# Unit 2's queries in halves, a cast on GpSimd, and the third and fourth piece of w_out ahead of v

## The chip, the cores and the metric

The kernel runs on one core of a Trainium2 chip. The metric is the device time of one execution in microseconds (us), taken as the median over runs. Engines are named as in the profile: PE (TensorE; PEld is its weight load), DVE (VectorE), ACT (ScalarE), POOL (GpSimd), SP (SyncE, which here only issues transfers).

## The reference

Two operators follow one another. The first is a recurrent retention over 4 batches, 8 heads, 768 steps, head size 64; the second is a feed-forward layer with a leaky rectifier over the 3072 x 512 result.

```python
state = gamma * state + einsum('bhd,bhe->bhde', k[:, :, t], v[:, :, t])
y[:, :, t] = scale * einsum('bhd,bhde->bhe', q[:, :, t], state)
...
h = x @ w_in                                             # 3072x512 @ 512x2048
g = np.maximum(h, 0.0) + alpha * np.minimum(h, 0.0)
return (g @ w_out).astype(np.float32)                    # 3072x2048 @ 2048x512
```

Inputs and output are float32.

## The kernel before

**Tiling.** Time is cut into units of 256 steps, three to a batch, twelve in all (u = 0 to 11). Two units make a block of 512 tokens, six in all (n = 0 to 5). The feed-forward layer works on blocks. All matmuls take float16.

**A unit.** `load` brings its k, q and v into staging tiles. `rescale` multiplies k (t = 0) and q (t = 1) with powers of the decay into the tile `kdq`; `cast_v` writes v as `vx`. `turn_pe(u, hh, bank)` transposes `kdq` for four of the eight heads (hh = 0: heads 0 to 3), four transposes of k and then four of q, and ACT copies the result to `kq` (line 236). `score_mm(u, hh, banks)` multiplies k with q into two banks, and `masks` writes the masked scores from there on DVE (line 482). `sum_mm` forms the unit's contribution to the state from `kdq` and `vx` (line 260). `state` adds it to the running state on DVE (`ss`), decays it on POOL (`tf`) and copies it to `tg` on POOL and ACT. `out_mm` forms y out of `tg` (line 500) and out of scores and `vx` (line 532), and `take_y` copies y as `xT`, the input of the feed-forward layer.

**A block.** `ffn1(n, ...)` multiplies `xT` with w_in into `hps` (line 629) and applies the rectifier on ACT and DVE (lines 640, 642). `ffn2(0, ..., parts=4)`, block 0's second product, multiplies the result with w_out into four banks (line 798). Both are generators: `tick(gen, m)` emits the next m matmuls, so matmuls of the layer stand between the steps of the units. `ffn2` has 64 matmuls. They go in four rounds over slices of four of w_out's sixteen row tiles; in each round every one of the four banks gets four matmuls. So matmuls 0 to 15 read row tiles 0 to 3, matmuls 16 to 31 read row tiles 4 to 7, where each group of four goes through the slice.

**w_in and w_out.** w_in comes in pieces of float32 (`get_wi`) which POOL casts (`cast_wi`). w_out's first half comes in four pieces of two row tiles, 512 KB each (`get_wo32(0)` to `(3)`), cast by `cast_wo(engine, i)` on the engine given. Pieces 2 and 3 land where w_in's columns of tiles 4 to 7 lay, so their loads wait until these are cast. The second half comes by transfers that POOL issues (`get_wo(2)`, `get_wo(3)`, line 971). The loads of unit 4's queries and everything behind them on SP wait for `get_wo(2)` to land.

**What sets the order.** The order is written out by hand in lines 986 to 1284: each engine runs its instructions in the order in which the program emits them, and waits at each for what it needs. All loads named above but `get_wo` are issued by SP, in program order, and each issue waits until its destination is free.

**Around the change.** While PE ends block 0's first product, POOL casts the last pieces of w_in, scales unit 2's k in two halves (27.64 to 29.68 us) and its q in one, and casts its v. Then PE goes through `tick(gen, 5)`, the turn of heads 0 to 3 of unit 2, six ticks, scores, the turn of heads 4 to 7, six ticks, scores, state sums, eight ticks, `out_mm(2)`, seven ticks, and goes on to `half`, block 1's first product (lines 1097 to 1124).

The loads of units 0 and 1 already come in halves, by part names such as "k0" and "k1": heads 0 to 3 and heads 4 to 7.

Of the kernel before, what the change touches and what calls it, by code (L numbers as in the profile page):

```python
# [22 lines left out]
def kernel(  # L23
# [76 lines left out]
    def ps(bank, name, dt=FP, n=512):  # L100
        return psp.tile([128, n], dt, tag=f"b{bank}", name=name)
# [27 lines left out]
    def hold(ins):  # L129
        if held:  # L130
            tc.add_manual_dep(
                ins.ins,
                held.pop().ins.name,
                mybir.DependencyInfo(
                    mybir.DependencyClass.Sync, mybir.DependencyReason.DATA
                ),
                reason="loads behind weights",
            )

    def rows(x):  # L140
        return slice(64 * x, 64 * x + 64)

    def load(u, parts="kqv"):
        if u >= NU:
            return
        b, c = divmod(u, UPB)
        t = staged.setdefault(u, {})
        for nm in parts:
            src = {"k": k, "q": q, "v": v}[nm[0]]
            if nm[0] not in t:  # L150
                t[nm[0]] = sbp.tile(
                    [128, H, 2 * D], FP, tag=f"{nm[0]}s", bufs=3, name=f"{nm[0]}s{u}"
                )
            h = slice(0, H) if len(nm) == 1 else slice(4 * int(nm[1]), 4 * int(nm[1]) + 4)
            if u >= SPLIT and nm != "q":
                for x in range(2):
                    for y in range(2):
                        at = U * c + 128 * x + 64 * y
                        nc.sync.dma_start(
                            out=t[nm][rows(x), :, D * y : D * y + D],  # L160
                            in_=src[b, :, at : at + 64, :].rearrange("h p d -> p h d"),
                        )
                continue
            hold(
                nc.sync.dma_start(  # L165
                    out=t[nm[0]][:, h, :],
                    in_=src[b, h, U * c : U * c + U, :].rearrange(
                        "h (p r) d -> p h (r d)", r=2
                    ),
                )  # L170
            )

    def unit(u):
        if u not in prepped:
            prepped[u] = (
                sbp.tile([128, 2, 2, H, D], F16, tag="kdq", bufs=3, name=f"kdq{u}"),
                sbp.tile([128, 4 * NP, 128], F16, tag="kq", bufs=3, name=f"kq{u}"),
                sbp.tile([128, H, 2, D], F16, tag="vx", bufs=3, name=f"vx{u}"),
            )
        return prepped[u]  # L180

    def rescale(eng, u, t, h0, h1):
        kdq = unit(u)[0]
        at = OQ if t else (O2 if u >= SPLIT else 0)
        return eng.tensor_tensor(  # L185
            out=kdq[:, t, :, h0:h1, :].rearrange("p r h d -> p h r d"),
            in0=staged[u]["kq"[t]][:, h0:h1, :].rearrange("p h (r d) -> p h r d", r=2),
            in1=tab[:, at + 2 * h0 : at + 2 * h1]
            .rearrange("p (h r) -> p h r", r=2)
            .unsqueeze(3)  # L190
            .to_broadcast([128, h1 - h0, 2, D]),
            op=MULT,
        )
# [28 lines left out]
    def turn_pe(u, hh, bank):  # L222

        kdq, kq, _ = unit(u)
        trb = ps(bank, "trb", F16, 1024)
        n = 0
        for t in range(2):
            for r in range(2):
                for p in (2 * hh, 2 * hh + 1):
                    nc.tensor.transpose(  # L230
                        out=trb[:, n : n + 128],
                        in_=kdq[:, t, r, 2 * p : 2 * p + 2, :].rearrange("p a d -> p (a d)"),
                        identity=ident,
                    )
                    n += 128
        nc.scalar.activation(  # L236
            out=kq.rearrange("p (x a) i -> p x a i", x=4)[:, :, 2 * hh : 2 * hh + 2, :],
            in_=trb.rearrange("p (x a i) -> p x a i", x=4, a=2),
            func=COPY,
            bias=0.0,  # L240
            scale=1.0,
        )

    def qmove(kq, a, c, p):
        return kq.rearrange("p (t r a) i -> p t r a i", t=2, r=2)[rows(a), 1, :, p, rows(c)]
# [207 lines left out]
    def score_mm(u, hh, banks):  # L453
        _, kq, _ = prepped[u]
        kv = kq.rearrange("p (t r a) i -> p t r a i", t=2, r=2)
        scs = [ps(banks[0], "sca"), ps(banks[1], "scb")]
        for r in range(2):
            for pp in range(2):
                p = 2 * hh + pp
                for c in range(2):  # L460
                    for a in range(2):
                        at, n, q = 256 * r + 128 * pp, 128, qmove(kq, a, c, p)
                        if u >= SPLIT and r == 1:
                            at, n, q = 256 + 64 * pp, 64, q[:, :, 32:64]
                        nc.tensor.matmul(  # L465
                            out=scs[a][rows(c), at : at + n],
                            lhsT=kv[rows(a), 0, r, p, rows(c)],
                            rhs=q,
                            start=True,
                            stop=True,  # L470
                        )
        live[u, hh] = scs

    def masks(u, hh, parts=(0, 1)):
        for a in parts:
            m2 = sbp.tile([128, 512], F16, tag=f"m2{a}{hh}", bufs=2, name=f"m2{a}{hh}")
            if u >= SPLIT:
                i = nc.vector.tensor_tensor(
                    out=m2[:, 0:384], in0=live[u, hh][a][:, 0:384], in1=mj, op=MULT
                )  # L480
            else:
                i = nc.vector.tensor_tensor(  # L482
                    out=m2.rearrange("p (r a i) -> p r a i", r=2, a=2),
                    in0=live[u, hh][a].rearrange("p (r a i) -> p r a i", r=2, a=2),
                    in1=mask.unsqueeze(2).to_broadcast([128, 2, 2, 128]),
                    op=MULT,
                )
            live[u, hh][a] = m2
        return i
# [458 lines left out]
    def tick(gen, m=10**6):  # L948
        for _ in range(m):
            if next(gen, 1) == 1:  # L950
                return
# [4 lines left out]
    def win_part(lo, hi):  # L956
        x, y = ((1, 0), (1, 1), (0, 0), (1, 0))[lo // 4]
        return early[x][:, y, :, 128 * (lo % 4) : 128 * (hi - lo + lo % 4)]
# [4 lines left out]
    def cast_wi(eng, lo, hi):  # L963
        o, i = w_in_all[:, :, 128 * lo : 128 * hi], win_part(lo, hi)
        if eng is nc.scalar:
            return eng.activation(out=o, in_=i, func=COPY, bias=0.0, scale=1.0)
        return eng.tensor_copy(out=o, in_=i)  # L967
# [5 lines left out]
    def wo_part(i):  # L973
        return early[i // 2][:, 1, 2 * (i % 2) : 2 * (i % 2) + 2, :]

    def get_wo32(i):
        nc.sync.dma_start(out=wo_part(i), in_=wo[:, 2 * i : 2 * i + 2, :])  # L977

    def cast_wo(eng, i):
        o, i = w_out_all[:, 2 * i : 2 * i + 2, :], wo_part(i)  # L980
        if eng is nc.scalar:
            return eng.activation(out=o, in_=i, func=COPY, bias=0.0, scale=1.0)
        return eng.tensor_copy(out=o, in_=i)  # L983


    V, G, A = nc.vector, nc.gpsimd, nc.scalar
# [79 lines left out]
    load(2, ("k0", "k1"))  # L1066
    get_wo32(0)
    get_wo32(1)
    load(2, ("q", "v"))
    score_mm(1, 1, (0, 1))  # L1070
    masks(1, 1)
    state(1, 1, V)
    gen = ffn1(0, (2, 3, 6, 7, 0, 1, 2, 3, 6, 7, 4, 5, 0, 1, 2, 3), apart=4)
# [2 lines left out]
    cast_wi(G, 6, 8)  # L1076
    get_wo32(2)
    get_wo32(3)
    cast_wi(G, 8, 10)
    cast_wi(G, 10, 12)  # L1080
    cast_wi(G, 12, 14)
    cast_wi(G, 14, 16)
    rescale(G, 2, 0, 0, 4)
    rescale(G, 2, 0, 4, 8)
    rescale(G, 2, 1, 0, 8)
    load(3, ("k", "q", "v"))
    cast_v(G, 2)
    out_mm(1, (4, 5), evict=False)
# [7 lines left out]

    gen = ffn2(0, (0, 1, 2, 3), parts=4)
    half = ffn1(1, (6, 7, 4, 5, 4, 6, 0, 1, 2, 3, 0, 4, 5, 6, 7, 1), apart=12)
    tick(gen, 5)
    turn_pe(2, 0, 5)  # L1100
    tick(gen, 6)
    score_mm(2, 0, (6, 7))
    masks(2, 0)
    cast_wo(V, 2)
    cast_wo(V, 3)
    wsum = sbp.tile([128, 4, HF, HM], F16, tag="wsum", name="wsum")
    turn_pe(2, 1, 4)
    tick(gen, 6)
    score_mm(2, 1, (6, 7))
    sum_mm(2, (5, 4))  # L1110
    state(2, 0, G, "ga")
# [6 lines left out]
    get_wo(3)  # L1118
    cast_v(G, 3)
    w_sums(0, 0, HF, G)  # L1120
    tick(gen, 8)
    out_mm(2, (4, 5))
    tick(gen, 7)
    tick(half, 24)
    turn_pe(3, 0, 6)
    tick(half, 8)
# [39 lines left out]
    for n in range(1, NBLK):  # L1166
        more = n + 1 < NBLK
        u0 = 2 * (n + 1)
        if n > 1:
            if more:  # L1170
                gen = ffn1(n, (7, 2, 3, 1, 0, 6, 5, 4, 7, 1, 0, 4, 5, 6, 7, 1))
            else:
                gen = ffn1_mixed(n, PLAN5, BANKS5)
# [21 lines left out]
        gen = ffn2_seven(n, 0, 1) if more else ffn2_seven(n, 0, 1, (2, 3, (4, 6)))  # L1195
# [119 lines left out]
```

## Time and profile before

| | |
|---|---|
| median of 3 runs | 201.85 us (201.05 to 202.13) |
| profiled execution | 200.61 us, of which span 198.6 us |
| PE busy | 189.7 us (95%) |
| DVE, ACT, POOL busy | 157.6, 115.1, 104.2 us |
| granted TensorE clock | 1.00 |
| HBM read, written | 27.31 MB, 6.29 MB |

The span is the time between the first and the last instruction of the profiled execution; the execution takes 2.0 us more. Times in the rows are us from the start of the span. In the order in time a row gives start, length, engine, line, operation, output and inputs, count, and in brackets the idle time of the engine ahead of it and what ended it. In a row on transfers stand the destination and source, the issuing queue, count, KB each, and the us from issue to landing. Matmuls are pipelined, so that the length of a row of matmuls reaches beyond the start of the next. DMA shares count the packets' own time.

### The profile page before, as it was taken

The page shows a single profiled execution, that of the slowest core. Times are in us where ns is not written, and L with a number is a line of the kernel's source. Part 1 is how long each engine was busy: PE and PEld are TensorE (multiplying, and loading weights), DVE is VectorE, ACT ScalarE, POOL GpSimd, SP SyncE. Part 2 cuts the span into 40 slices and gives each one's busy share as a digit, 9 for nine tenths or more (in the row PEclk, how much of TensorE's full clock was granted, in tenths as well). Part 3 has the DMA queues.
Part 4 walks back from the last instruction along what each step waited for, and adds up shares of the span by engine and source line. Part 5 has one row for each costly group of instructions (what it writes and reads, how often), then busy time and mean ns, then how long its engine had stood idle before and what let it go on. Part 6 is the DMA issues. An engine that isn't in the chain of part 4 may idle for free.

```text
span 198.6 us, 6058 instructions
## 1 busy us (share of the span) xinstructions
PE 189.7 (95%) x2517; PEld 127.8 (64%) x2517; DVE 157.6 (79%) x261; ACT 115.1 (58%) x198; POOL 104.2 (52%) x110
## 2 busy tenths in 40 slices
PE   6788997999999999999999999999999999999993
PEld 2456543468458598744688644688644788865882
DVE  7798986626698998289989289987389998899983
ACT  4465665338267568466557567467467476678110
POOL 3298685099468634981067990076970181039300
PEclk9999999999999999999999999999999999999999
DMA  5999999987969998899897999918966010400014
GB/s 160 324 328 338 376 375 331 323 164 124 237 144 243 262 174 224 201 314 231 170 220 182 306 187 216 237 59 220 270 111 131 17 56 3 158 3 0 0 61 150
DMA packets 90009, 37.90 MB, mean 191 GB/s; under 512 B 57968, under 2 KB 87680, under 8 KB 89984
## 3 DMA queue, kind: packets, MB, share of 16 engines
q1 hardware_dynamic: 88752, 36.45, 69.8%
q0 software_dynamic: 1056, 1.05, 3.5%
q8 instruction: 19, 0.31, 0.6%
q10 hardware_dynamic: 176, 0.04, 0.2%
q14 instruction: 6, 0.05, 0.1%
HBM read 27.31 MB, written 6.29 MB: 169 GB/s over the span
## 4 chain that ended last, share of the span: by engine, by line
PE 83%; DVE 5%; DMA 4%; SPq 3%; ACT 1%; POOL 1%; issue 1%; DVEq 0%
PE hps L629 28%; PE ox L846 16%; PE oy L846 13%; PE ops L798 6%; DMA qs<-in_q_dram 4%; PE hps L712 3%; PE sp L752 3%; DVE m L482 2%; PE kps L106 2%; SPq L165 2%; PE y L532 1%; PE sca L465 1%; PE st L284 1%; POOL kdq L185 1%; PE trb L230 1%; SPq L977 1%
## 5 line engine op out<-in xcount | busy, mean ns | idle before, releaser
L629 PE MATMUL hps<-xT,win 128*128 128x512 f16 (+1 forms) x384 | 70.9, 344 | 0.3 <-POOL win L967 0.3
L642 DVE SCALAR_TENSOR_TENSOR gt<-hm,oma,hps 128x512 f16<-128x512 f32 (+1 forms) x96 | 59.1, 656 | 13.6 <-ACT hm L640 5.1
L640 ACT ACTIVATE hm<-hps 128x512 f32<-128x512 f32 x80 | 47.4, 596 | 25.2 <-PE hps L629 22.8
L629 PEld LDWEIGHTS <-win 128*128 128x128 f16 x384 | 37.1, 98 | 31.8 <-POOL win L967 0.8
L846 PEld LDWEIGHTS <-gs 128*128 128x128 f16 x320 | 31.0, 98 | 3.7
L846 PEld LDWEIGHTS <-gt 128*128 128x128 f16 x240 | 22.9, 98 | 4.2
L185 POOL TENSOR_TENSOR kdq<-qs,tab 128x1024 f16<-128x1024 f32 (+1 forms) x11 | 20.0, 1822 | 5.7 <-DMA qs<-in_q_dram 3.4
L333 POOL CAST tg<-tm 64x256 f16<-64x256 f32 x12 | 4.8, 396 | 33.6 <-DVE tm L301 22.6
L185 POOL TENSOR_TENSOR kdq<-ks,tab 128x1024 f16<-128x1024 f32 (+1 forms) x12 | 20.2, 1686 | 3.6 <-PE y L514 2.6
L555 ACT ACTIVATE xT<-y 128x512 f16<-128x512 f32 x22 | 14.9, 743 | 4.6 <-PE y L532 3.4
L846 PE MATMUL ox<-wout,gt 128*128 128x256 f16 x144 | 17.3, 273 | 0.0
L846 PE MATMUL oy<-wsum,gs 128*128 128x256 f16 x144 | 17.2, 273 | 0.0
L798 PE MATMUL ops<-wout,gt 128*128 128x512 f16 x64 | 15.5, 380 | 0.4 <-DVE wout L983 0.4
L201 POOL CAST vx<-vs 128x1024 f16<-128x1024 f32 (+1 forms) x13 | 12.6, 970 | 5.3 <-DMA vs<-in_v_dram 5.3
L612 DVE TENSOR_TENSOR gs<-gt 128x1024 f16<-128x1024 f16 (+1 forms) x14 | 13.0, 934 | 0.2
L236 ACT ACTIVATE kq<-trb 128x1024 f16<-128x1024 f16 x8 | 8.2, 1023 | 7.0 <-PE trb L230 7.0
L866 ACT ACTIVATE cu<-oy 128x512 f32<-128x512 f32 x10 | 6.0, 597 | 10.7 <-PE oy L846 10.1
L313 POOL TENSOR_TENSOR tf<-ss,tab 128x256 f32<-128x256 f32 x10 | 10.3, 1028 | 2.5 <-DVE ss L312 1.5
L662 POOL TENSOR_SCALAR hn<-qc,oma 128x256 f32<-128x256 f32 x4 | 4.5, 1140 | 12.5 <-DVE qc L774 12.4
L423 POOL TENSOR_TENSOR tf<-ss,tab 128x256 f32<-128x256 f32 x6 | 5.8, 974 | 9.6 <-DVE ss L422 9.6
L870 DVE TENSOR_TENSOR os<-ox,cu 128x512 f32<-128x512 f32 x5 | 3.4, 686 | 9.1 <-PE ox L846 9.1
L967 POOL CAST win<-early 128x1024 f16<-128x1024 f32 (+1 forms) x9 | 8.8, 975 | 2.4 <-DMA early<-in_moe_w_in_dram 2.2
(118 smaller groups left out, 289.7 us busy)
## 6 DMA issues: line engine op xcount, KB each, us to landing
qs<-in_q_dram SPq DMA_DIRECT2D x10, 512.0 KB, 5.1
ks<-in_k_dram SPq DMA_DIRECT2D x32, 128.0 KB, 3.5
vs<-in_v_dram SPq DMA_DIRECT2D x32, 128.0 KB, 4.3
early<-in_moe_w_in_dram SPq DMA_DIRECT2D x7, 512.0 KB, 8.3
out_dram<-os SPq DMA_DIRECT2D x9, 256.0 KB, 2.7
early<-in_moe_w_out_dram SPq DMA_DIRECT2D x4, 512.0 KB, 6.7
out_dram<-ot SPq DMA_DIRECT2D x4, 512.0 KB, 4.1
ks<-in_k_dram SPq DMA_DIRECT2D x6, 256.0 KB, 4.9
```

Of the source, the lines that this page charges most:

```text
L185: return eng.tensor_tensor(out=kdq[:, t, :, h0:h1, :].rearrange("p r h d -> p h r d"), in0=staged[u]["kq"[t]][:, h0:h1, :].rearrange("p h ...
L201: eng.tensor_copy(out=o, in_=i)
L236: nc.scalar.activation(out=kq.rearrange("p (x a) i -> p x a i", x=4)[:, :, 2 * hh : 2 * hh + 2, :], in_=trb.rearrange("p (x a i) -> p x a ...
L313: nc.gpsimd.tensor_tensor(out=t, in0=ss, in1=dec, op=MULT)
L555: nc.scalar.activation(out=o, in_=i, func=COPY, bias=0.0, scale=1.0,)
L612: last_g.append(nc.vector.tensor_tensor(out=o, in0=a, in1=b, op=op))
L629: nc.tensor.matmul(out=hps[:, f, :].rearrange("p (u t) -> p u t", t=U), lhsT=w_in_all[:, hp, 128 * (f0 + f) : 128 * (f0 + f) + 128], rhs=x ...
L640: nc.scalar.activation(out=hm, in_=hps, func=RELU, bias=0.0, scale=-1.0)
L642: nc.vector.scalar_tensor_tensor(out=gt[:, f0 + f, U * lo : U * hi], in0=hm[:, f, :], scalar=oma_sb[:, f0 + f : f0 + f + 1], in1=hps[:, f, :],
L798: nc.tensor.matmul(out=opss[tq], lhsT=gt[:, ft, 128 * tq : 128 * tq + 128], rhs=w_out_all[:, ft, :], start=(ft == 0), stop=(ft == NFT - 1),)
L846: nc.tensor.matmul(out=o[1][m], lhsT=lhs(f, m), rhs=rhs(f), start=(first and f == 0 and (m == 0 or o[0] is None)), stop=(f == HF - 1), ski ...
L967: return eng.tensor_copy(out=o, in_=i)
```

## The change

Unit 2's queries are loaded as two transfers of four heads each, and scaled on POOL as two instructions of four heads each. Unit 2's v is loaded behind pieces 2 and 3 of w_out. Piece 3 is cast on POOL, between the scaling of unit 2's queries and the cast of its v; piece 2 stays on DVE and is cast ahead of unit 2's first masks. Block 0's second product gives eight matmuls, in place of five, ahead of unit 2's first turn; five in place of six ahead of the second scores; seven in place of eight ahead of `out_mm(2)`; and six in place of seven behind it.

```diff
     get_wo32(0)
     get_wo32(1)
-    load(2, ("q", "v"))
+    load(2, ("q0", "q1"))
     score_mm(1, 1, (0, 1))
...
     get_wo32(2)
     get_wo32(3)
+    load(2, "v")
     cast_wi(G, 8, 10)
...
     rescale(G, 2, 0, 4, 8)
-    rescale(G, 2, 1, 0, 8)
+    rescale(G, 2, 1, 0, 4)
+    rescale(G, 2, 1, 4, 8)
+    cast_wo(G, 3)
     load(3, ("k", "q", "v"))
     cast_v(G, 2)
...
-    tick(gen, 5)
+    tick(gen, 8)
     turn_pe(2, 0, 5)
     tick(gen, 6)
     score_mm(2, 0, (6, 7))
+    cast_wo(V, 2)
     masks(2, 0)
-    cast_wo(V, 2)
-    cast_wo(V, 3)
     wsum = sbp.tile([128, 4, HF, HM], F16, tag="wsum", name="wsum")
     turn_pe(2, 1, 4)
-    tick(gen, 6)
+    tick(gen, 5)
     score_mm(2, 1, (6, 7))
...
     w_sums(0, 0, HF, G)
-    tick(gen, 8)
+    tick(gen, 7)
     out_mm(2, (4, 5))
-    tick(gen, 7)
+    tick(gen, 6)
     tick(half, 24)
```

## The prediction

> **What bounds the kernel now.** I read the page first, then the busy time by stretches, then the order in time of each engine around the lines of the change, then the transfers one by one.
>
> ```profile
> span 198.6 us, 6058 instructions
> PE 189.7 (95%) x2517; PEld 127.8 (64%) x2517; DVE 157.6 (79%) x261; ACT 115.1 (58%) x198; POOL 104.2 (52%) x110
> ```
>
> ```profile
> 44.00:60.00 16.00, 16.00 (x204) 10.45 (x203) 11.99 (x21) 9.41 (x16) 11.20 (x7) 1.00 0.85 172
> 60.00:198.60 138.60, 135.23 (x1840) 96.15 (x1837) 113.26 (x187) 82.31 (x148) 67.08 (x68) 1.00 0.65 157
> ```
>
> The columns of the second view are the stretch, its length, and the busy time of PE, its weight load, DVE, ACT and POOL, then clock, DMA share and GB/s. PE is the bound: it is busy for all of 44 to 60 us and for all but 3.4 us of the rest, at a granted clock of 1.00. So time comes back only where PE stands still before 44 us. The order in time of PE (start, length, line, operation, count, idle before it) shows where, at the place of the change:
>
> ```profile
> 32.37 0.39 PE L230 MATMUL trb<-mi,kdq 128*128 128x128 f16 x4
> 34.18 0.40 PE L230 MATMUL trb<-mi,kdq 128*128 128x128 f16 x4 [1.43 <-POOL kdq L185]
> ...
> 36.16 0.62 PE L230 MATMUL trb<-mi,kdq 128*128 128x128 f16 x8
> 36.61 1.24 PE L798 MATMUL ops<-wout,gt 128*128 128x512 f16 x5
> 38.21 0.38 PE L798 MATMUL ops<-wout,gt 128*128 128x512 f16 x1 [0.36 <-DVE wout L983]
> 38.52 0.24 PE L465 MATMUL sca<-kq 64*64 64x128 f16 x1
> ...
> 38.76 0.42 PE L260 MATMUL st<-vx,kdq 64*64 64x64 f16 x16
> 39.11 1.90 PE L798 MATMUL ops<-wout,gt 128*128 128x512 f16 x8
> 40.85 0.61 PE L500 MATMUL y<-kq,tg 128*128 128x128 f16 x8
> 41.39 0.64 PE L532 MATMUL y<-m,vx 64*64 64x128 f16 x32
> ...
> 43.48 2.78 PE L629 MATMUL hps<-xT,win 128*128 128x256 f16 x24
> ```
>
> Lengths of matmuls overlap, so I reckon from start to start. Eight product matmuls take 40.85 - 39.11 = 1.74, that is 0.2175 each; eight transposes take 36.61 - 36.16 = 0.45. The two stalls are then: the query transposes of unit 2 start at 34.18 where 32.37 + 0.22 = 32.59 was due, **1.59 lost**; the sixth matmul starts at 38.21 where 36.61 + 5 x 0.2175 = 37.70 was due, **0.51 lost**, waiting for DVE's cast of w_out's piece 2. Together 2.10 us, and nothing more can be won here.
>
> What the first stall waits for is POOL, and POOL waits for a transfer:
>
> ```profile
> 27.64 2.04 POOL L185 TENSOR_TENSOR kdq<-ks,tab 128x512 f16<-128x512 f32 x2
> 32.23 1.90 POOL L185 TENSOR_TENSOR kdq<-qs,tab 128x1024 f16<-128x1024 f32 x1 [2.55 <-DMA qs<-in_q_dram]
> 34.07 1.04 POOL L201 CAST vx<-vs 128x1024 f16<-128x1024 f32 x1
> 39.79 0.61 POOL L423 TENSOR_TENSOR tf<-ss,tab 128x256 f32<-128x256 f32 x1 [4.68 <-DVE ss L422]
> 40.47 0.39 POOL L451 CAST tg<-tf 64x256 f16<-64x256 f32 x1
> ```
>
> The transfers, each as its issue and its time from issue to landing, with the chain's row for the queries:
>
> ```profile
> 18.89 2.50 SPq L165 DMA_DIRECT2D ks<-in_k_dram  x1
> ks<-in_k_dram SPq DMA_DIRECT2D x1, 256.0 KB, 8.4
> 21.44 1.24 SPq L165 DMA_DIRECT2D ks<-in_k_dram  x1
> ks<-in_k_dram SPq DMA_DIRECT2D x1, 256.0 KB, 6.6
> 24.61 7.55 DMA qs<-in_q_dram
> 25.66 1.78 SPq L165 DMA_DIRECT2D vs<-in_v_dram  x1
> vs<-in_v_dram SPq DMA_DIRECT2D x1, 512.0 KB, 8.0
> 27.55 3.14 SPq L977 DMA_DIRECT2D early<-in_moe_w_out_dram  x1
> early<-in_moe_w_out_dram SPq DMA_DIRECT2D x1, 512.0 KB, 7.4
> 30.73 0.47 SPq L977 DMA_DIRECT2D early<-in_moe_w_out_dram  x1
> early<-in_moe_w_out_dram SPq DMA_DIRECT2D x1, 512.0 KB, 5.5
> ```
>
> Landings: the two halves of k at 27.3 and 28.0, q at 32.16, v at 33.7, w_out's pieces 2 and 3 at 34.95 and 36.2. They come one behind the other in the order of issue, each 512 KB of q or v taking 1.5 of the stream and each piece 1.3, while a transfer needs 5.5 to 8.4 from issue to landing. The stream is full, so order in it is what counts.
>
> **The change part by part.**
>
> *Queries in halves.* The same bytes go, so the second half lands when q did, 32.16. The first lands half of 1.5 earlier, 31.41; the halves of k show that a half takes half, 0.7 apart. POOL starts 0.07 behind a landing (32.23 against 32.16) and a half of k's scaling takes 2.04 / 2 = 1.02: the first half is scaled from 31.48 to 32.50, the second to 33.52, in all 0.14 us more POOL work than the whole in one, and the end still 0.6 earlier than 34.13. Turning heads 0 to 3 needs only the first half.
>
> The Trainium skill, "DMA: Bandwidth & Descriptors" (section "Anatomy of one DMA"), speaks against this part: measured on GpSimd's queue, it gives every transfer a fixed part of about 2.0 us beside its bytes. The halves of k, 0.7 apart, disagree as far as a full queue goes: the fixed part overlaps. What the rule would make of the time stands beside the second rival.
>
> *Eight matmuls ahead instead of five.* Three more take 3 x 0.2175 = 0.65, so the transposes begin at 32.37 + 0.65 = 33.02 and those of the queries at 33.24, 0.74 behind their scaling: **the 1.59 go**. The three are not extra: 8 + 6 + 5 + 7 + 6 = 32 as 5 + 6 + 6 + 8 + 7 = 32. They read pieces 0 and 1 only. The second turn of unit 2 then begins at 36.16 - 1.59 + 0.65 = 35.22, when its queries (33.52) have long been there, and the five matmuls behind it run from 35.67 to 36.76.
>
> *w_out's pieces ahead of v.* Without v before them they land at 32.16 + 1.3 = 33.45 and 34.75, and v at 34.75 + 1.5 = 36.25. Two casts change places and engine:
>
> ```profile
> 36.27 0.69 DVE L482 TENSOR_TENSOR m<-sca,mi 128x512 f16<-128x512 f32 x1 [3.10 <-PE scb L465]
> 36.88 0.68 DVE L482 TENSOR_TENSOR m<-scb,mi 128x512 f16<-128x512 f32 x1
> 37.47 1.28 DVE L983 CAST wout<-early 128x1024 f16<-128x1024 f32 x2
> ```
>
> DVE was idle for 3.10 ahead of unit 2's first masks, so piece 2's cast (half of 1.28) goes there at 33.5 to 34.2. Its price is nothing, and it would cost its 0.64 only with a landing after some 34.6, since the masks are due at 36.27 - 0.94 = 35.33. They end 37.56 - 36.16 = 1.40 behind the start of the second turn, at 36.62, ahead of the next scores in the same banks. Piece 3 goes to POOL: a cast of that shape there took 1.04 (v's row), 34.82 to 35.86. The last of the five matmuls reads it, at 35.67 + 4 x 0.2175 = 36.54, 0.7 later. **The 0.51 go as well.**
>
> *What waits in their place.* First the scores, for ACT's copy of the turned unit:
>
> ```profile
> 36.81 1.02 ACT L236 ACTIVATE kq<-trb 128x1024 f16<-128x1024 f16 x1 [1.17 <-PE trb L230]
> ```
>
> The copy ended 37.83 - 36.16 = 1.67 behind the start of its turn, so 36.89; PE follows ACT by 0.07 (as hps at 43.48 follows xT below), so the scores start at 36.96. Matmul to scores is 38.52 - 38.21 = 0.31 rather than 0.22, so they could have at 36.85: **0.11 lost**. Second, v: POOL casts it behind piece 3, from 36.25 + 0.07 to 37.36, and PE follows POOL by 0.05 (34.18 against 34.13), so the state sums start at 37.41 instead of 36.96 + 0.24 = 37.20: **0.21 lost**, a new wait of PE. Behind v's cast POOL has unit 2's `tf`, which is due only 1.03 after the sums and loses nothing.
>
> Third, the ticks taken from behind were cover. The sums' way over DVE, POOL and ACT to `tg` took 40.86 - 38.76 = 2.10. PE had eight matmuls over it; with seven it comes to y at 0.35 + 1.52 = 1.87, its first four matmuls need nothing new, the others could start at 2.14 and may at about 2.17: 0.03. The last row of cover is ACT's, at the turn from y to hps:
>
> ```profile
> 42.07 1.34 ACT L555 ACTIVATE xT<-y 128x512 f16<-128x512 f32 x2 [1.22 <-PE y L532]
> ```
>
> From the 32 y matmuls to hps it was 43.48 - 41.39 = 2.09, and xT ended at 43.41, 0.07 ahead of that. So with six matmuls there instead of seven hps still needs 2.09: **0.22 lost**.
>
> Sum: 1.59 + 0.51 - 0.11 - 0.21 - 0.03 - 0.22 = **1.53 won**, with the same 32 matmuls done when hps begins, at some 41.95 for 43.48. Counted the other way: 37.41 + 1.87 + 0.57 + 2.09 = 41.94.
>
> Bounds: if all new waits vanished, 2.1. Below, every term hangs on v's landing: beyond 36.0 each microsecond that it is later costs one. Its place in the stream is fixed by the bytes, but spacings of 1.3 to 1.5 over four transfers can be off by 0.5 in all; that gives 1.0. I take 1.5, since the bytes ahead of v's end are just those that were ahead of piece 3's end at 36.2.
>
> **The rivals.**
>
> *SP's issue holds v up.* The largest issue above is piece 2's, 3.14, and the profile puts 2.2 of that to POOL's scaling of k:
>
> ```profile
> SPq L977 <- POOL kdq L185: 2.2, 1, 2.2
> ```
>
> The scaling of k ends at 29.68 and does not move. If that wait is real, v, now behind both pieces, can't be issued before 30.73 + 0.47 = 31.20. With piece 3's 5.5 to landing that is 36.7: 0.45 less, 1.1 won, 200.8. With v's own 8.0 it is 39.2: cast by 40.3, sums at 40.35, hps 4.53 behind at 44.9, **1.4 slower, 203.3**. The point from which this is a loss is a landing of v at 37.8, since sums at 38.95 give hps at 43.48. For it speaks only that row; against it, that v's 8.0 was time behind k, two pieces and q in a full stream, and that the cast of w_in which piece 2 must wait for precedes the scaling of k on POOL.
>
> *A half costs the queue as much as a whole.* Then q takes 3.0 instead of 1.5, v lands at 37.75 and nothing is won, 201.8: the new wait for v takes the place of both old ones. The halves of k, 0.7 apart, are against it. By the Trainium skill's 2.0 per transfer ("DMA: Bandwidth & Descriptors", "Anatomy of one DMA") an estimate is v at 38.25 and 0.45 slower, which nothing in these rows bears out.
>
> *Won here and lost later.* What PE reaches 1.5 earlier may not be ready: unit 3's scaled k and q, and the loads of units 4 and 5 behind POOL's load of w_out. Most of it moves along, as POOL comes free 1.3 earlier; and PE has no idle time from 44 to 60 us. But rows without a wait don't tell how near one is. If all is eaten: 201.85.
>
> **How the numbers follow.** The profiled execution took 200.61 with a span of 198.6, so 2.0 lie around it; 1.5 less is 197.1 and 199.1. It stands below the timed runs (201.05 to 202.13), so I take the 1.5 from their median: 201.85 - 1.5 = **200.35**, with 199.9 to 200.9 as the forecast's own range. Chances: the forecast 0.58; v late and some 1.0 or less won 0.17, about 200.8 to 201.4; no change, by the half's price or by a loss later, 0.15, 201.8; slower by late v 0.10, 203.3. For the range of eight in ten I reach to 199.7 below (all new waits gone) and 202.0 above. About 0.5%, 1.0 us, is what a measurement here can tell from no change. The forecast lies beyond it nearly always (0.55) and v somewhat late in some (0.07): faster 0.62; slower 0.10; the same 0.28.
>
> **What would show it.** Right: PE's query transposes within 33.1 to 33.4 with no idle ahead of them; POOL's scaling as two pieces of about 1.04, the first from 31.5; no wait of the product on a cast of w_out; a wait of PE for v's cast of about 0.2 ahead of the state sums near 37.4; hps at about 42.0. Wrong: v landing after 37, which shows as a long wait of the sums on POOL; a transposes' wait still there, if the first half lands with the second; or an idle PE between 42 and 75 us that was not there before.

## The result

The changed kernel takes 199.43 us in the median of 16 runs (198.62 to 200.88), the kernel before, run beside it, 200.95 (200.14 to 202.31, 16 runs). The ratio is **0.9928, interval 0.9903 to 0.9953**: 0.7% faster, 1.45 us. The forecast was 1.5 us less, which as a ratio is 0.9926. But it was set from a base of 201.85, and the kernel before ran at 200.95: 199.43 lies below the lower end of the stated range, 199.7.

The profiled execution took 198.62 us, with a span of 196.8. PE in order of time, in the changed kernel (start, length, line, operation, tiles, count):

```profile
31.06 2.10 PE L798 MATMUL ops<-wout,gt 128*128 128x512 f16 x8
33.00 0.61 PE L230 MATMUL trb<-mi,kdq 128*128 128x128 f16 x8
33.45 1.46 PE L798 MATMUL ops<-wout,gt 128*128 128x512 f16 x6
...
35.19 0.62 PE L230 MATMUL trb<-mi,kdq 128*128 128x128 f16 x8
35.64 1.24 PE L798 MATMUL ops<-wout,gt 128*128 128x512 f16 x5
...
37.17 0.42 PE L260 MATMUL st<-vx,kdq 64*64 64x64 f16 x16
37.52 1.69 PE L798 MATMUL ops<-wout,gt 128*128 128x512 f16 x7
39.04 0.74 PE L500 MATMUL y<-kq,tg 128*128 128x128 f16 x8
39.71 0.64 PE L532 MATMUL y<-m,vx 64*64 64x128 f16 x32
40.28 1.47 PE L798 MATMUL ops<-wout,gt 128*128 128x512 f16 x6
41.77 2.78 PE L629 MATMUL hps<-xT,win 128*128 128x256 f16 x24
```

Both stalls are gone: all eight transposes of the first turn stand in one row with no idle time, and no product matmul behind the second turn waits for a cast. From the first product matmul to hps it is 41.77 - 31.06 = 10.71 us, where it was 43.48 - 31.29 = 12.19: **1.48 less in the stretch that the prediction summed to 1.53**. This holds for these two profiles; a second pair, further below, splits the gain otherwise. Behind the stretch nothing moved: 155.0 from hps to the end, 155.1 before.

```profile
44.00:60.00 16.00, 16.00 (x204) 10.48 (x202) 12.26 (x23) 10.11 (x18) 11.06 (x8) 1.00 0.86 188
60.00:196.80 136.80, 133.43 (x1824) 94.56 (x1822) 112.53 (x185) 80.71 (x144) 65.60 (x68) 1.00 0.63 155
```

PE's idle time behind 60 us is 3.37, as it was. POOL and DVE in the same stretch of the changed kernel:

```profile
30.07 2.49 POOL L185 TENSOR_TENSOR kdq<-qs,tab 128x512 f16<-128x512 f32 x2 [1.79 <-DMA qs<-in_q_dram]
33.41 1.07 POOL L983 CAST wout<-early 128x1024 f16<-128x1024 f32 x1 [0.85 <-DMA early<-in_moe_w_out_dram]
34.89 1.04 POOL L201 CAST vx<-vs 128x1024 f16<-128x1024 f32 x1 [0.42 <-DMA vs<-in_v_dram]
38.19 0.61 POOL L423 TENSOR_TENSOR tf<-ss,tab 128x256 f32<-128x256 f32 x1 [2.26 <-DVE ss L422]
```

```profile
30.63 1.02 DVE L983 CAST wout<-early 128x1024 f16<-128x1024 f32 x1
31.58 1.39 DVE L642 SCALAR_TENSOR_TENSOR gt<-hm,oma,hps 128x512 f16<-128x512 f32 x2
32.90 0.68 DVE L983 CAST wout<-early 128x1024 f16<-128x1024 f32 x1
```

Two things are not as reckoned. The whole stream of loads ran ahead: POOL begins the queries at 30.07, where 31.48 was foreseen, and v's cast ends at 35.93, so that the state sums at 37.17 don't wait for it. And DVE's cast of w_out's piece 1, 0.69 us long before, took 1.02, while POOL's two halves took 2.49 in place of 2.04. The experiments turn on this.

### The profile page after: what moved, and what is told of

Its sections match the earlier page's. It is cut to its first block, busy times and chain, and to the rows that moved or that the text cites. A ratio compares the mean times of both kernels' runs of the same rounds, so it can differ in the third digit from the quotient of the medians.

```text
span 196.8 us, 6060 instructions
## 1 busy us (share of the span) xinstructions
PE 189.8 (96%) x2517; PEld 127.8 (65%) x2517; DVE 157.2 (80%) x260; ACT 115.1 (59%) x198; POOL 105.8 (54%) x112
## 4 chain that ended last, share of the span: by engine, by line
PE 88%; SPq 4%; DMA 3%; DVE 1%; ACT 1%; POOL 1%; issue 1%
PE hps L629 34%; PE ox L846 16%; PE oy L846 13%; PE ops L798 7%; SPq L165 4%; PE hps L712 4%; PE sp L752 3%; DMA early<-in_moe_w_in_dram 3%; PE y L532 1%; PE trb L230 1%; PE st L284 1%; PE sca L465 1%; PE ov L846 1%; PE oz L846 1%; PE ow L846 1%; POOL win L967 1%
## 5 line engine op out<-in xcount | busy, mean ns | idle before, releaser
L846 PEld LDWEIGHTS <-gt 128*128 128x128 f16 x240 | 22.8, 98 | 4.2
L185 POOL TENSOR_TENSOR kdq<-qs,tab 128x1024 f16<-128x1024 f32 (+1 forms) x12 | 20.6, 1723 | 5.3 <-DMA qs<-in_q_dram 3.0
L798 PEld LDWEIGHTS <-gt 128*128 128x128 f16 x64 | 5.8, 97 | 6.5 <-issue 0.7
```

Source lines behind the costliest of these rows:

```text
L185: return eng.tensor_tensor(out=kdq[:, t, :, h0:h1, :].rearrange("p r h d -> p h r d"), in0=staged[u]["kq"[t]][:, h0:h1, :].rearrange("p h ...
L798: nc.tensor.matmul(out=opss[tq], lhsT=gt[:, ft, 128 * tq : 128 * tq + 128], rhs=w_out_all[:, ft, :], start=(ft == 0), stop=(ft == NFT - 1),)
L846: nc.tensor.matmul(out=o[1][m], lhsT=lhs(f, m), rhs=rhs(f), start=(first and f == 0 and (m == 0 or o[0] is None)), stop=(f == HF - 1), ski ...
```

## The experiments

**Each part alone.** First only the halves:

```diff
-    load(2, ("q", "v"))
+    load(2, ("q0", "q1", "v"))
-    rescale(G, 2, 1, 0, 8)
+    rescale(G, 2, 1, 0, 4)
+    rescale(G, 2, 1, 4, 8)
```

> Only the queries of unit 2 in halves, loads and scaling; the matmuls, the casts and v stay where they were before. Theory (the sum of the prediction): with five matmuls ahead, the query transposes are due at 32.59 and their scaling is done at about 32.50, so the whole first stall of 1.59 us goes, while the 0.51 us ahead of the sixth matmul stay, since DVE casts piece 2 behind the masks. Time before minus 1.6 us, nearly all that the whole change brings (1.45 measured). Rival (the halves alone don't do it, the three matmuls moved ahead must cover the scaling): 0.3 to 0.9 us of the transposes' wait stay, time before minus 0.7 to 1.3.

199.61 us, ratio 0.9935 (0.9907 to 0.9964): 1.3 us faster. PE with the halves alone:

```profile
33.13 0.61 PE L230 MATMUL trb<-mi,kdq 128*128 128x128 f16 x8
...
37.37 0.38 PE L798 MATMUL ops<-wout,gt 128*128 128x512 f16 x1 [0.35 <-DVE wout L983]
```

With five matmuls ahead there is no wait for the queries any more, and the second stall is still there. The halves alone carry most of the gain; in this profile the three matmuls ahead are not needed for it.

Second, only the matmuls' distribution, 8, 6, 5, 7, 6:

```diff
-    tick(gen, 5)
+    tick(gen, 8)
     turn_pe(2, 0, 5)
...
     turn_pe(2, 1, 4)
-    tick(gen, 6)
+    tick(gen, 5)
...
-    tick(gen, 8)
+    tick(gen, 7)
     out_mm(2, (4, 5))
-    tick(gen, 7)
+    tick(gen, 6)
```

> Only the 32 matmuls distributed 8, 6, 5, 7, 6 in place of 5, 6, 6, 8, 7; queries whole, casts and loads as before. Theory: the transposes' wait shrinks from 1.59 to 0.94 us, but the matmuls behind the second turn now read piece 3 as well, which DVE has cast only at 38.75, so that the scores come at about 39.1 in place of 38.5 and the cover taken from behind is missing: hps 0.4 us later than before, time before plus 0.4. Rival (the matmuls moved ahead are what wins): time before minus 0.65 us.

201.9 us, ratio 1.0043 (1.0012 to 1.0074): 0.9 slower, the way the theory had it and twice its size. PE, DVE and POOL of this kernel say why:

```profile
31.34 0.59 PE L798 MATMUL ops<-wout,gt 128*128 128x512 f16 x2
33.36 1.46 PE L798 MATMUL ops<-wout,gt 128*128 128x512 f16 x6 [1.42 <-DVE wout L983]
34.65 0.61 PE L230 MATMUL trb<-mi,kdq 128*128 128x128 f16 x8
...
38.89 0.98 PE L798 MATMUL ops<-wout,gt 128*128 128x512 f16 x3 [1.00 <-DVE wout L983]
```

```profile
30.91 2.40 DVE L983 CAST wout<-early 128x1024 f16<-128x1024 f32 x1
```

```profile
30.86 1.90 POOL L185 TENSOR_TENSOR kdq<-qs,tab 128x1024 f16<-128x1024 f32 x1 [2.56 <-DMA qs<-in_q_dram]
```

The queries landed earlier than in the first profile, so POOL began to scale them 0.05 ahead of DVE's cast of piece 1. The cast then took 2.40 in place of 0.69 and ended 0.55 behind POOL's end at 32.76. PE stood for it at its third product matmul. The matmuls moved ahead stand behind that one, so they cover nothing here. Further on the missing cover is lost: the wait for the cast of piece 2 costs 38.89 - (37.29 + 2 x 0.2175) = 1.16 where it cost 0.51, and the way from the sums to hps some 0.3 more.

Third, only the order of the loads and the casts:

```diff
-    load(2, ("q", "v"))
+    load(2, "q")
...
     get_wo32(3)
+    load(2, "v")
...
     rescale(G, 2, 1, 0, 8)
+    cast_wo(G, 3)
...
+    cast_wo(V, 2)
     masks(2, 0)
-    cast_wo(V, 2)
-    cast_wo(V, 3)
```

> Only w_out's pieces 2 and 3 ahead of v and the two casts in their new places; queries whole, matmuls 5, 6, 6, 8, 7. Theory: the wait of the sixth matmul on its cast goes (0.51 us), the wait of the query transposes (1.59) stays, v's cast ends at about 37.4 and the state sums are due at 38.25, so that v costs nothing. Time before minus 0.5 us. Rival (a later v costs at once, or the cast on GpSimd delays what is behind it): time before, or up to 0.5 us more.

200.01 us, ratio 0.9972 (0.9948 to 0.9996): 0.56 faster, as the theory had it, with no wait of the sixth matmul. The first stall stands at the third matmul here too, behind a cast of 2.35 beside POOL's scaling from 30.64:

```profile
33.15 0.81 PE L798 MATMUL ops<-wout,gt 128*128 128x512 f16 x3 [1.38 <-DVE wout L983]
```

```profile
30.74 2.35 DVE L983 CAST wout<-early 128x1024 f16<-128x1024 f32 x1
```

**The kernel before once more**, for its profile.

> The kernel before, once more, for its profile. The profile of the changed kernel had the transfers of unit 2's k landing 1.4 us earlier (25.9 and 26.7 in place of 27.3 and 28.1) although nothing ahead of them was changed. Theory: the pace of the load stream differs from execution to execution by 1 to 2 us and so does the kernel before, which waits for it: here the queries land anywhere from 30 to 32.2, the stall at the transposes is 0 to 0.5 us shorter for an early landing and the span follows. Rival: the pace is the kernel's own, the queries land at 32.2 again and the span is 198.6 within 0.3.

200.29 us, span 198.3. POOL began the queries at 31.61, and PE's stall is 0.60 idle in place of 1.43:

```profile
33.93 0.40 PE L230 MATMUL trb<-mi,kdq 128*128 128x128 f16 x4 [0.60 <-POOL kdq L185]
```

```profile
31.42 0.69 DVE L983 CAST wout<-early 128x1024 f16<-128x1024 f32 x1
```

```profile
31.61 2.25 POOL L185 TENSOR_TENSOR kdq<-qs,tab 128x1024 f16<-128x1024 f32 x1 [2.56 <-DMA qs<-in_q_dram]
```

This time DVE came first by 0.19: its cast has its 0.69, and POOL's scaling takes 2.25 in place of 1.90. So the pace differs between executions of one kernel, and with it the size of the stall: 33.93 where 32.93 + 0.22 = 33.15 was due, 0.78 lost in place of 1.59. The span came out only 0.3 lower, which the rival's 198.6 within 0.3 allows as well, since PE came to its first product matmul 0.57 later (31.86 for 31.29).

**Do the two engines shut each other out?** That DVE's cast and an instruction of POOL can't run at the same time is called the lock from here on. Three edits at piece 1's cast test it. On the kernel before, the cast on ACT:

```diff
-    cast_wo(V, 1)
+    cast_wo(A, 1)
```

> The kernel before with one edit: w_out's piece 1 cast on ACT in place of DVE. In the profiles of the two single-part kernels with whole queries, DVE's cast of piece 1 took 2.40 and 2.35 us in place of 0.69, just as long as POOL's scaling of the queries went on beside it, and PE stood 1.6 us at the third matmul for it. Theory (DVE's cast and POOL's scaling shut each other out, so the loss before is the same 1.5 us in another place whenever the queries land before 31): ACT's cast ends at about 32.2, PE loses 0.6 there in place of 1.6, and the kernel is 0.5 to 1.0 us faster than before; POOL's scaling takes 1.9 with no stretch. Rival (the cast was slow for a reason of its own): no gain, and up to 0.5 slower since ACT's cast is 0.4 us longer and holds up the rectifier of the last two tiles.

199.96 us, ratio 0.9961 (0.9940 to 0.9982): 0.8 faster. PE waits 0.35 for ACT's cast, and POOL's scaling from 31.06 takes 1.90:

```profile
32.53 0.81 PE L798 MATMUL ops<-wout,gt 128*128 128x512 f16 x3 [0.35 <-ACT wout L982]
```

```profile
31.06 1.90 POOL L185 TENSOR_TENSOR kdq<-qs,tab 128x1024 f16<-128x1024 f32 x1 [2.57 <-DMA qs<-in_q_dram]
```

On the kernel before, the cast on POOL itself, ahead of the queries:

```diff
+    cast_wo(G, 1)
     rescale(G, 2, 1, 0, 8)
...
-    cast_wo(V, 1)
```

> The kernel before with one edit: w_out's piece 1 cast on POOL ahead of its scaling of the whole queries, in place of DVE. Theory (in most executions what PE loses before is DVE's cast held up by POOL's scaling, not the scaling itself): piece 1 is cast by 30.4 to 31.1, the queries are scaled by 32.5 to 33.0 and are due at about 32.7 to 33.1, so 1.0 to 1.4 us faster than before, nearly what the halves alone bring; where the queries land only at 32.2, as in the profile before, the wait of the transposes stays and nothing is won. Rival (the lock is not what costs): no gain.

199.76 us, ratio 0.9946 (0.9918 to 0.9973): 1.1 faster, by the move of one line. POOL:

```profile
30.13 1.04 POOL L983 CAST wout<-early 128x1024 f16<-128x1024 f32 x1 [1.05 <-DMA early<-in_moe_w_out_dram]
31.64 1.90 POOL L185 TENSOR_TENSOR kdq<-qs,tab 128x1024 f16<-128x1024 f32 x1 [0.48 <-DMA qs<-in_q_dram]
```

On the changed kernel, DVE's cast one rectifier step earlier:

```diff
-    tick(gen, 65)
+    tick(gen, 61)
+    cast_wo(V, 1)
+    tick(gen, 4)
     cast_wo(A, 0)
-    cast_wo(V, 1)
```

> The changed kernel with DVE's cast of w_out's piece 1 one rectifier step (0.75 us) earlier, so that it begins ahead of POOL's scaling of the queries. Theory (the two shut each other out; the cast of 1.03 us in place of 0.69 made PE lose 0.21 at the third matmul): the cast takes 0.69, POOL's first half is stretched instead, which the 0.7 us of margin there cover, and the kernel is 0.2 us faster than the changed one, before minus 1.65. Rival (the cast must wait for the piece to land and holds up the rectifier): 0 to 0.4 slower than the changed kernel.

199.28 us, ratio 0.9928 (0.9902 to 0.9954): the changed kernel's own, so the rival's time, but not by its reason. DVE and POOL in order of time:

```profile
30.16 1.50 DVE L983 CAST wout<-early 128x1024 f16<-128x1024 f32 x1
```

```profile
30.07 2.49 POOL L185 TENSOR_TENSOR kdq<-qs,tab 128x512 f16<-128x512 f32 x2 [1.82 <-DMA qs<-in_q_dram]
```

The piece and the queries had both landed, POOL was 0.09 ahead again, and the cast, now 1.50, ended at 31.66, where it ended without the edit (30.63 + 1.02 = 31.65). Two of the three edits won what the lock gives by the theory. The third didn't bring the cast ahead of POOL, so its gain stays untested; its profile, with POOL first and the cast stretched, agrees with the lock.

**Does v cost what it is late?** The changed kernel with v behind unit 3's k and q:

```diff
-    load(2, "v")
...
-    load(3, ("k", "q", "v"))
+    load(3, ("k", "q"))
+    load(2, "v")
+    load(3, "v")
```

> The changed kernel with unit 2's v loaded still later, behind unit 3's k and q. It then lands where unit 3's v landed, at about 37.8 to 38.0 in place of 34.8, and its cast ends at 39.0. Theory (every microsecond of v beyond the state sums' own time costs one): the sums start at 39.05 in place of 37.17, and the kernel is 1.9 us slower than the changed one, 0.4 slower than the one before. Rival (the sums have slack): the time of the changed kernel, before minus 1.45.

201.21 us, ratio 1.0028 (0.9999 to 1.0057): some 2.0 slower than the changed kernel by the two ratios, and 0.56 above the one before, which the interval just doesn't tell from nothing. PE:

```profile
39.47 0.44 PE L260 MATMUL st<-vx,kdq 64*64 64x64 f16 x16 [1.60 <-POOL vx L201]
39.84 2.55 PE L798 MATMUL ops<-wout,gt 128*128 128x512 f16 x7
```

The wait that the slower rival named is real once v is late enough: the sums start at 39.47 where 36.17 + 1.53 = 37.70 was due, 1.77 lost. In this profile PE also ran slower behind it, of which below; so not all of the 2.0 need be the wait. Four of the twelve executions show a granted clock of 0.991 or 0.992 and took 202.28 to 205.54. The other eight have their median at 200.9, 1.5 above 0.9928 x 200.83 = 199.4, the changed kernel's time by its ratio.

Then the other way, v ahead of pieces 2 and 3 again, in the loads and on POOL:

```diff
-    load(2, ("q0", "q1"))
+    load(2, ("q0", "q1", "v"))
...
-    load(2, "v")
...
-    cast_wo(G, 3)
     load(3, ("k", "q", "v"))
     cast_v(G, 2)
+    cast_wo(G, 3)
```

> The changed kernel with v back ahead of w_out's pieces 2 and 3, in the loads and on POOL (v's cast ahead of piece 3's). Theory: at the pace of the load stream that most profiles show (second half of the queries at 30.8 to 31.3), v lands at 32.3 to 32.8, piece 3 at 34.9 to 35.4, is cast by 36.0 to 36.5 and is due at about 36.5 to 37.0, so that the order of these loads is worth nothing: the time of the changed kernel, within 0.3, that is before minus 1.3 to 1.9. Rival (the order is needed, as the prediction reckoned it at the pace of the profile before): the fifth matmul waits 0.8 us for piece 3's cast, 0.8 slower than the changed kernel, before minus 0.6 to 1.0.

199.12 us, ratio 0.9928 (0.9900 to 0.9956): the time of the changed kernel. POOL cast piece 3 from 35.16 to 36.20, and the fifth matmul, which reads it, started at 36.01 + 4 x 0.2175 = 36.88. At this pace the order of the loads is worth nothing, and the places of the two casts are what removes the second stall. Whether the order is worth something at the pace of the first profile is not shown: that pace wasn't met again.

**The cover.** The changed kernel with the matmuls as 6, 6, 6, 7, 7:

```diff
-    tick(gen, 8)
+    tick(gen, 6)
     turn_pe(2, 0, 5)
...
     turn_pe(2, 1, 4)
-    tick(gen, 5)
+    tick(gen, 6)
...
     out_mm(2, (4, 5))
-    tick(gen, 6)
+    tick(gen, 7)
```

> The changed kernel with the 32 matmuls as 6, 6, 6, 7, 7 in place of 8, 6, 5, 7, 6. Theory (two matmuls too many stand ahead of the first turn, and the turn from y to hps and the second scores lack one each as cover): 0.2 to 0.3 us faster than the changed kernel, before minus 1.7; the wait of hps for xT goes, the query transposes still find their scaling done. Rival (the first turn needs the cover of eight): 0.2 to 0.4 slower than the changed kernel.

198.81 us, ratio 0.9913 (0.9885 to 0.9941). Its profile has no wait ahead of the transposes:

```profile
31.48 1.52 PE L798 MATMUL ops<-wout,gt 128*128 128x512 f16 x6
32.84 0.61 PE L230 MATMUL trb<-mi,kdq 128*128 128x128 f16 x8
...
41.76 2.78 PE L629 MATMUL hps<-xT,win 128*128 128x256 f16 x24
```

The stretch from the first product matmul to hps is 41.76 - 31.48 = 10.28, 0.4 less than in the changed kernel. Of that 0.11 is gained at the second scores and 0.19 ahead of hps; the rest is a shorter wait at the third matmul, since PE came there later in this execution. The same with piece 1's cast on POOL as well, beside the changed kernel on one chip:

```diff
+    cast_wo(G, 1)
     rescale(G, 2, 1, 0, 4)
     rescale(G, 2, 1, 4, 8)
...
-    cast_wo(V, 1)
```

> The changed kernel with the 32 matmuls as 6, 6, 6, 7, 7, and w_out's piece 1 cast on POOL ahead of its scaling of the queries, in place of DVE. Theory (DVE's cast and POOL's scaling shut each other out, and one after the other on POOL they can't): piece 1 lands at 29.3, is cast by 30.4, the queries are scaled by 31.5 and 32.5, no wait at the third matmul: 0.1 to 0.3 us faster than with 6, 6, 6, 7, 7 alone, before minus 1.9. Rival (DVE's cast costs nothing any more there): the time of that kernel, before minus 1.75.

> The changed kernel once more, beside the kernel that gives the 32 matmuls as 6, 6, 6, 7, 7 with the cast on POOL, on one chip. Theory: 0.9928 of the kernel before again, within 0.9905 and 0.995; in its profile the part from block 0's first product matmul to hps takes 10.5 to 10.8 us, and hps to the end 155.0 to 155.3, so that what differs between executions lies ahead of it. Rival (the ratio of the first measurement was a matter of the chip): a ratio outside that interval.

198.98 us at a ratio of 0.9902 (0.9871 to 0.9933), and 199.0 at 0.9908 (0.9881 to 0.9936) for the changed kernel itself. The stretch took 42.24 - 32.03 = 10.21 and 41.87 - 31.22 = 10.65. So the waits that the even distribution is to remove are gone, 0.3 in the profiles, but in whole runs no version is told apart from the changed kernel.

## Why the prediction was wrong, point by point

**What failed is the last step, the base.** "I take the 1.5 from their median: 201.85" put three runs above the profiled execution's own 200.61. Sixteen runs of the kernel before have their median at 200.95, and later groups at 200.73, 200.83, 201.10 and 200.55. Taken from the profiled execution the same sum gives 199.1, from the median of sixteen 199.4; measured, 199.43. The range was built round the same base, so it missed with it: its lower end, 199.7, is the base less the whole 2.1 of both stalls, and leaves nothing for a base that is itself off. That the profiled execution lay outside the three runs was seen, and should have widened the range downward by the difference.

What makes executions differ lies at least in part ahead of the change, as four profiles show (us; the fourth column is the stretch that the prediction summed):

| profile | POOL begins the queries | first product matmul | from there to hps | hps to the end | span |
|---|---|---|---|---|---|
| before | 32.23 | 31.29 | 12.19 | 155.1 | 198.6 |
| before, again | 31.61 | 31.86 | 11.36 | 155.1 | 198.3 |
| changed | 30.07 | 31.06 | 10.71 | 155.0 | 196.8 |
| changed, again | 30.16 | 31.22 | 10.65 | 155.1 | 196.9 |

The second pair gives 11.36 - 10.65 = 0.71 in the stretch, and 31.86 - 31.22 = 0.64 ahead of it, where profiles with and without the change lie mixed. So the agreement of 1.48 with 1.53 belongs to the profile from which the sum was made, and is in part luck. What holds in every pair is when hps starts: at 43.48 and 43.22 before, at 41.77 and 41.87 in the changed kernel, 1.35 to 1.71 earlier.

Over all profiles the first product matmul started at 31.06 to 32.16, and hps to the end took 155.0 to 155.4. Why the stream of loads runs at another pace is open; the slower and the faster of the timed executions have no profile.

**Both stalls, 2.10 won: right for the profile that was read.** The whole change removes them, the halves alone the first, the casts' new places alone the second. In the second profile of the kernel before they cost 0.78 + 0.51.

**The reason for the first stall was half of it.** The prediction put all 1.59 on the late queries, which is what the first profile shows. In the two kernels above with whole queries (only the distribution, only the order), where POOL began at 30.86 and 30.64, 1.59 and 1.54 were lost at the third matmul instead, since POOL's scaling shut out DVE's cast of piece 1. The first profile showed none of it, as the queries landed after the cast. The loss goes with the halves either way: the transposes wait for a half, and the cast was held up by a half at most (1.50 for 0.69 at the worst). What is left is 0.20 at the third matmul of the changed kernel: the first eight take 33.00 - 31.06 = 1.94, not 1.74. This term was missing.

**"Eight matmuls ahead": not needed for the gain.** The halves alone have no wait there with five, and the changed kernel with six had none either. Alone, the distribution costs 0.9.

**New waits.** The scores: start to start, the five matmuls and the wait for ACT's copy take 37.17 - 35.64 = 1.53 to the state sums, foreseen without v 1.53 (37.20 - 35.67). V's 0.21 was not paid, as the stream ran ahead; the kernel with v behind unit 3's k and q shows that it is paid when v is late. From the sums to y it was 1.87, as foreseen. The second half of y waited more than the 0.03: 39.71 - 39.04 = 0.67 for 0.54, 0.13 lost. From the y matmuls to hps 2.06, foreseen 2.09, so one matmul of cover was lost there, and the even distribution gets it back in the profile.

So the terms are 2.10 - 0.20 (lock, not foreseen) - 0.11 (scores) - 0.13 (y) - 0.19 (xT: 2.06 less the 1.87 that six matmuls give) = 1.47, against 1.48 measured in the first pair of profiles. That the total came so near to 1.53 is luck in one place: the 0.21 for v that was foreseen and not paid stands against the 0.20 of the lock that was paid and not foreseen.

**The rivals.** *SP's issue holds v up*: not so. In the changed kernel SP issued piece 2 from 25.39 to 26.03, before POOL began to scale k at 26.23, and v at 26.59, while POOL was still at it till 28.3. So the 2.2 that the row gave to POOL was no wait for that scaling; what held SP up in the profile before stays open.

```profile
25.39 0.64 SPq L977 DMA_DIRECT2D early<-in_moe_w_out_dram  x1
```

```profile
26.23 2.04 POOL L185 TENSOR_TENSOR kdq<-ks,tab 128x512 f16<-128x512 f32 x2
```

*A half costs the queue as much as a whole*: not so. Issue and landing of the first half, and of v:

```profile
23.21 1.00 SPq L165 DMA_DIRECT2D qs<-in_q_dram  x1
qs<-in_q_dram SPq DMA_DIRECT2D x1, 256.0 KB, 6.8
26.59 0.79 SPq L165 DMA_DIRECT2D vs<-in_v_dram  x1
vs<-in_v_dram SPq DMA_DIRECT2D x1, 512.0 KB, 8.2
```

The first half lands at 30.0 and v at 34.8, 4.8 later, with the second half, two pieces and v between: 0.75 + 2 x 1.3 + 1.5 = 4.85 if a half takes half. The fixed 2.0 us per transfer of the Trainium skill ("DMA: Bandwidth & Descriptors", "Anatomy of one DMA"), which it gives for GpSimd's queue, does not add up in this full queue of SP. *Won here and lost later*: not so, 155.0 behind hps.

## What to carry to other kernels

A sum over one stretch of a profile gives a difference, and that difference can come near while the time is off by 1 us: take it from a base of many runs, or give it as a ratio, and let the range hold the spread of the base. When a transfer's pace moves a stall, look at what else starts at that moment: some 1.6 us stood at the transposes in one profile, and at a cast in two kernels that load and scale the queries alike. Cutting a long instruction in halves helped both, as it bounds what anyone waits for.

## What the runs showed of the hardware that was not expected

**DVE's cast and POOL's instructions exclude each other.** A cast of 128x1024 from float32 to float16 in SBUF takes DVE 0.69 us alone. Beside a POOL scaling that began 0.05 to 0.10 earlier it took 2.40 and 2.35 (whole queries), and 1.50 beside a half that began 0.09 earlier. Each time it ended about 0.55 behind POOL's instruction. Where DVE began first, POOL was stretched: 2.25 for 1.90. DVE's rectifier steps, with one operand in PSUM, were not stretched and stretched nothing: in the profile before, POOL's two k halves took 2.04 beside them and each step its 0.75. The Trainium skill says just this ("SBUF — State Buffer", section "Who interferes with whom"): a copy or cast in DVE's two-port mode takes the ports that it shares with GpSimd, whoever comes first holds them for the whole instruction, and the other waits. The runs agree, though no view names the mode of a cast; the prediction had not drawn on it.

**PE at a lower clock behind a wait.** In the run with v late, PE was busy for 0.86 of the 2.50 us ahead of 39.5 (the columns as above: stretch, length, the five engines, clock, DMA):

```profile
37.00:39.50 2.50, 0.86 (x21) 0.34 (x21) 0.11 (x1) 0.39 (x1) 1.04 (x1) 1.00 1.05 281
39.50:44.00 4.50, 4.50 (x63) 2.78 (x62) 1.62 (x3) 0.41 (x1) 3.40 (x4) 0.62 0.44 83
```

In the next 4.5 us the granted clock was 0.62, and seven product matmuls took from 39.84 to 42.18, 2.34 in place of 1.52. The drop was not at once: in finer steps the clock is 1.00 up to 40.2 and half from 40.6 to 43.5, all the while PE is busy.

```profile
40.60:43.50 2.90, 2.90 (x29) 1.60 (x31) 0.96 (x2) 0.41 (x1) 2.81 (x4) 0.50 0.16 32
```

The idle times of 1.38 to 1.43 us in the other profiles were followed by no such drop. It is one profile; the granted clock over a whole execution is 0.991 or 0.992 in four of this kernel's twelve timed executions, and not below 0.997 in any execution of the other kernels. That the wait sets it off is not shown, and where the bound lies is open.
